# Dims-first q and k, tile-grouped recurrence products, ScalarE leaky ReLU and exponent clip in a RetNet plus feed-forward kernel

## The chip, the cores and the metric

The kernel runs on one core of a Trainium2 chip. The metric is the device time of one execution in microseconds (us). The time before the change is 878.79 us, the median of three runs (878.74 to 880.75).

## The reference

```python
B, H, S, D = 4, 8, 768, 64           # q, k, v: (B, H, S, D), float32
gamma = 1.0 - 2.0 ** (-5.0 - np.arange(H)); scale = 1.0 / np.sqrt(D)
for t in range(S):
    state = gamma[None, :, None, None] * state + np.einsum('bhd,bhe->bhde', k[:, :, t], v[:, :, t])
    y[:, :, t] = scale * np.einsum('bhd,bhde->bhe', q[:, :, t], state)
x = y.transpose(0, 2, 1, 3).reshape(B * S, H * D)   # 3072 x 512
h = x @ w_in                                        # w_in 512 x 2048, float64
g = np.maximum(0.01 * h, h)
out = (g @ w_out).astype(np.float32)                # w_out 2048 x 512, float64
```

## The kernel before

The recurrence goes by chunks of 128 tokens. A group is the same chunk `c` (0 to 5) of all four batches `b`, 512 tokens. A block, written (c, b) here, is one chunk of one batch, eight heads. The feed-forward of group c has 32 units `u` on TensorE: 16 units of `unit_h` (L200: four 128x512 products with `win`, each of which the trace shows as two passes) and 16 units of `unit_o` (L213: four parts of four products with `wout` for each batch). Between the units of group c runs the recurrence of group c + 1, one block every seven units: the decays at s = 0 (L87), the transposes at s = 1 (L98), the scores at s = 3 (L112), the outputs and the state at s = 5 (L130, L133, L141). The recurrence of group 0 stands ahead of everything.

A block does this. GpSimd multiplies q by g^t/sqrt(D) and v by g^-t. TensorE transposes q and k (four transposes each), ScalarE copies `qt` and VectorE copies `kt` out of PSUM. Eight score products use half of the array's rows each (64 dims of one head), in pairs, `a0p` and `a1p`. VectorE multiplies both results with the causal mask (`am`, L117). `yp` gets, for each of four head pairs, one 128x128 product with the block-diagonal state `st` (L130), then two products of 64 output columns with `am` (L133). ScalarE copies `yp` into `xt`. Four 128x128 products `sp` (L141) update the state, of which VectorE uses the two diagonal halves.

The weights come as float64 bits and are rounded to float32 on the chip in 32 pieces of 128x512 (16 of `win`, 16 of `wout`; p0 to p31 here). A piece takes five VectorE operations (`e` L179, `m` L186, `f` L188, `e` again L190, the result L192) and two GpSimd ones between the first and second `e` (L181, L183: clip, then shift and scale the exponent). Two pieces are rounded in each block of group 0, one behind each `unit_h` of group 0, and the last eight ahead of the `unit_o` parts that read them. The load of piece n + 4 is issued behind piece n.

The leaky ReLU of a unit is a ScalarE product with 0.01 (`low`, L203) and a VectorE maximum (`gt`, L204). All loads are issued by SyncE in program order; the scheduler is manual, so each engine runs its instructions in the order of the code. PSUM has four buffers for the recurrence (`att`), two for `hp`, two for `op`.

Of the kernel before, what the change touches and what calls it, by code (L numbers as in the profile page):

```python
# [10 lines left out]
FP32 = mybir.dt.float32  # L11
I32 = mybir.dt.int32
# [5 lines left out]
C = 128  # tokens of a chunk of the recurrence  # L18
# [3 lines left out]
def kernel(  # L22
    ctx: ExitStack,
    tc: tile.TileContext,
    q: bass.AP,
    k: bass.AP,
    v: bass.AP,
    w_in: bass.AP,
    w_out: bass.AP,
    decay: bass.AP,  # L30
    out: bass.AP,
):
# [11 lines left out]
    B, H, S, D = q.shape  # L44
    NC = S // C
    DM = H * D
    DF = w_in.shape[1]
# [4 lines left out]
    W = 512  # columns of a piece of the weights  # L52
# [14 lines left out]
    # The states of two heads, one beside the other on the diagonal; zero off it.  # L67
    st = [const.tile([128, HP, 128], FP32, name=f"st{b}") for b in range(B)]

    nc.sync.dma_start(out=dec, in_=decay)  # L70
    gq = dec[:, 0:H]
    gk = dec[:, H : 2 * H]
    gc = dec[:, 2 * H :]

# [1 line left out]
    heads = {}  # L76

    def load(c, b):
        t = [work.tile([128, H, D], FP32, tag=n, bufs=4, name=f"{n}_{c}_{b}") for n in "qkv"]
        for x, src in zip(t, (q, k, v)):  # L80
            nc.sync.dma_start(out=x, in_=src[b, :, ds(c * C, C), :].rearrange("h t d -> t h d"))
        heads[c, b] = t

    def decay_qv(c, b):
        qs, _, vs = heads[c, b]
        for x, g in ((qs, gq), (vs, gk)):
            nc.gpsimd.tensor_tensor(out=x, in0=x, in1=g.unsqueeze(2).to_broadcast([128, H, D]),  # L87
                                    op=ALU.mult)

    turned = {}  # L90

    def stage_t(c, b):
        qs, ks, _ = heads[c, b]
        got = []
        for x, n, copy in ((qs, "qt", nc.scalar.copy), (ks, "kt", nc.vector.tensor_copy)):
            ps = psum.tile([128, HP, C], FP32, tag="att", bufs=4, name=f"{n}p_{c}_{b}")
            for a in range(HP):
                nc.tensor.transpose(ps[:, a, :], x[:, 2 * a : 2 * a + 2, :], ident)  # L98
            t = work.tile([128, HP, C], FP32, tag=n, name=f"{n}_{c}_{b}")
            copy(out=t, in_=ps)  # L100
            got.append(t)
        turned[c, b] = got
# [3 lines left out]
    def stage_a(c, b):  # L106
        qt, kt = turned[c, b]
        ps = [psum.tile([128, HP, C], FP32, tag="att", bufs=4, name=f"a{j}p_{c}_{b}")
              for j in range(2)]
        for a in range(HP):  # L110
            for j in range(2):
                nc.tensor.matmul(ps[j][:, a, :], lhsT=kt[ts(j, 64), a, :],  # L112
                                 rhs=qt[ts(j, 64), a, :])
# [9 lines left out]
    def stage_y(c, b, xt):  # L123
        _, ks, vs = heads.pop((c, b))
        qt, _ = turned.pop((c, b))
        am = scores.pop((c, b))
        yp = psum.tile([128, HP, C], FP32, tag="att", bufs=4, name=f"yp_{c}_{b}")
        for a in range(HP):
            if c > 0:
                nc.tensor.matmul(yp[:, a, :], lhsT=st[b][:, a, :], rhs=qt[:, a, :],  # L130
                                 start=True, stop=False, skip_group_check=True)
            for j in range(2):
                nc.tensor.matmul(yp[ts(j, 64), a, :], lhsT=vs[:, 2 * a + j, :],  # L133
                                 rhs=am[j][:, a, :], start=(c == 0), stop=True,
                                 skip_group_check=True)
        nc.scalar.copy(out=xt[:, :, ts(b, C)], in_=yp)  # L136
        if c == NC - 1:
            return
        sp = psum.tile([128, HP, 128], FP32, tag="att", bufs=4, name=f"sp_{c}_{b}")
        for a in range(HP):  # L140
            nc.tensor.matmul(sp[:, a, :], lhsT=ks[:, 2 * a : 2 * a + 2, :],  # L141
                             rhs=vs[:, 2 * a : 2 * a + 2, :])
        for j in range(2):
            half = st[b][ts(j, 64), :, ts(j, 64)]
            new = sp[ts(j, 64), :, ts(j, 64)]
            if c > 0:
                nc.vector.tensor_tensor(out=half, in0=half, in1=new, op=ALU.add)  # L147
            nc.vector.tensor_tensor(
                out=half, in0=half if c > 0 else new,
                in1=gc[ts(j, 64)].unsqueeze(2).to_broadcast([64, HP, D]), op=ALU.mult)  # L150

# [1 line left out]
    pieces = [(w_in[ts(i, 128), ts(r, W)], win[r][i]) for r in range(DF // W) for i in range(KIN)]  # L153
    pieces += [(w_out[ts(f, 128), :], wout[f]) for f in range(KOUT)]
    first_out = KIN * (DF // W)
    raws = {}
    LOW, HIGH = 896 << 20, 1151 << 20  # float64 exponent fields of float32's 0 and 255

    def load_piece(n):
        if w_in.dtype == FP32:  # L160
            nc.sync.dma_start(out=pieces[n][1], in_=pieces[n][0])
            return
        raws[n] = work.tile([128, W], I64, tag="raw", bufs=4, name=f"raw{n}")
        nc.sync.dma_start(out=raws[n], in_=pieces[n][0])

# [6 lines left out]
    def round_words(n):  # L172
# [23 lines left out]
    def unit_h(c, f, xt):  # L196
# [27 lines left out]
    for b in range(B):  # L224
# [95 lines left out]
```

## Time and profile before

| | |
|---|---|
| median of three runs | 878.79 us |
| span of the profiled execution | 878.3 us |
| TensorE busy | 824.0 us (94%) |
| VectorE, ScalarE, GpSimd busy | 244.1, 99.5, 109.0 us |
| mean granted TensorE clock | 0.97 |
| DMA moved | 42.39 MB |

The span is the time from the first to the last instruction of the profiled execution. The median of the runs is 0.5 us longer than it. A busy TensorE is not TensorE at its peak: the records of its instructions overlap, so in the rows below the distance from start to start tells what an instruction costs. The program falls into stages: the recurrence of group 0 (to 52.8 us), the 16 `unit_h` of group 0 (to 127.6), its `unit_o` (to 229.6), and then groups 1 to 5, which are alike but for the end.

### The profile page before, as it was taken

What the parts mean: (1) busy time and instruction counts of PE and PEld (TensorE: products, weight loads), DVE (VectorE), ACT (ScalarE), POOL (GpSimd) and SP (SyncE); (2) the same over time, 40 slices, a digit from 0 to 9 for tenths busy, and PEclk for the clock granted to TensorE, in tenths of its full rate; (3) what the DMA queues carried; (4) which work ended last, traced back from release to release, by engine and by line L of the source; (5) the groups of instructions that cost most, each with busy time, mean ns of one, the idle gap of its engine ahead of it and who ended that gap; (6) DMA issues with size and microseconds to landing.
All of it is one profiled execution on the core that took longest, in us unless ns stands there. A gap on an engine that the chain in (4) does not pass through costs nothing.

```text
span 878.3 us, 6856 instructions
## 1 busy us (share of the span) xinstructions
PE 824.0 (94%) x2816; PEld 407.9 (46%) x2816; DVE 244.1 (28%) x405; ACT 99.5 (11%) x169; POOL 109.0 (12%) x119
## 2 busy tenths in 40 slices
PE   4579886699999999999999999999999999999998
PEld 3445342155455555454555454554444444444443
DVE  5878886711022211022211022210022100021000
ACT  1111110000111100111100011100011100011100
POOL 4443543620000000000000000000000000000000
PEclk9899997589999999999999999999999999999999
DMA  9864442211010111010110101110100000000000
GB/s 222 221 156 127 126 136 92 60 48 49 25 24 13 36 42 43 28 33 13 36 37 26 47 13 36 37 37 24 49 0 1 1 12 13 24 1 0 1 24 24
DMA packets 83118, 42.39 MB, mean 48 GB/s; under 512 B 75920, under 2 KB 75920, under 8 KB 83088
## 3 DMA queue, kind: packets, MB, share of 16 engines
q1 hardware_dynamic: 79632, 35.67, 16.5%
q10 hardware_dynamic: 3456, 6.29, 1.9%
q8 instruction: 22, 0.36, 0.2%
q14 instruction: 8, 0.07, 0.0%
HBM read 35.66 MB, written 6.29 MB: 48 GB/s over the span
## 4 chain that ended last, share of the span: by engine, by line
PE 83%; DVE 8%; POOL 5%; DMA 1%; issue 1%; SPq 1%; ACT 0%; POOLq 0%
PE op L213 37%; PE hp L200 32%; PE yp L133 4%; PE yp L130 3%; POOL e L183 3%; PE sp L141 2%; POOL e L181 2%; PE a0p L112 2%; DVE e L190 2%; PE qtp L98 1%; DVE win L192 1%; DVE wout L192 1%; DVE e L179 1%; PE ktp L98 1%; DVE gt L204 1%
## 5 line engine op out<-in xcount | busy, mean ns | idle before, releaser
L213 PE MATMUL op<-wout,gt 128*128 128x512 f32 x768 | 346.4, 607 | 16.5 <-DVE wout L192 16.5
L200 PE MATMUL hp<-xt,win 128*128 128x512 f32 x768 | 338.5, 596 | 0.0
L213 PEld LDWEIGHTS op<-wout,gt 128*128 128x128 f32 x768 | 145.2, 193 | 195.7 <-issue 166.9
L200 PEld LDWEIGHTS hp<-xt,win 128*128 128x128 f32 x768 | 144.0, 191 | 171.5 <-issue 169.1
L204 DVE TENSOR_TENSOR gt<-low,hp 128x512 f32<-128x512 f32 x96 | 65.9, 687 | 325.2 <-ACT low L203 325.1
L203 ACT ACTIVATE low<-hp 128x512 f32<-128x512 f32 x96 | 57.3, 597 | 301.8 <-PE hp L200 297.9
L87 POOL TENSOR_TENSOR v<-v,dec 128x512 f32<-128x512 f32 x24 | 27.7, 1153 | 266.9 <-DMA v<-in_v_dram 266.9
L133 PE MATMUL yp<-am,v 128*64 128x128 f32 x384 | 45.3, 321 | 15.8 <-DVE am L117 15.5
L87 POOL TENSOR_TENSOR q<-q,dec 128x512 f32<-128x512 f32 x24 | 28.1, 1172 | 156.1 <-DMA q<-in_q_dram 155.7
L217 ACT COPY ob<-op 128x512 f32<-128x512 f32 x24 | 14.1, 586 | 254.8 <-PE op L213 254.8
L147 DVE TENSOR_TENSOR st<-st,sp 64x256 f32<-64x256 f32 x32 | 13.4, 418 | 94.6 <-PE sp L141 94.4
L130 PE MATMUL yp<-qt,st 128*128 128x128 f32 x160 | 38.2, 321 | 0.0
L130 PEld LDWEIGHTS yp<-qt,st 128*128 128x128 f32 x160 | 26.3, 195 | 20.9 <-issue 20.9
L133 PEld LDWEIGHTS yp<-am,v 128*64 128x64 f32 x384 | 22.9, 148 | 27.6 <-issue 17.1
L117 DVE TENSOR_TENSOR am<-a0p,mask 128x512 f32<-128x512 f32 x24 | 16.5, 687 | 69.1 <-PE a1p L112 69.1
L100 DVE COPY kt<-ktp 128x512 f32<-128x512 f32 x24 | 16.5, 687 | 62.8 <-PE ktp L98 62.8
L181 POOL TENSOR_SCALAR e<-e 128x512 uint32<-128x512 uint32 x32 | 23.0, 719 | 86.8 <-DVE e L179 86.7
L112 PEld LDWEIGHTS a0p<-qt,kt 64*128 64x128 f32 x192 | 23.9, 193 | 20.1 <-issue 16.4
L112 PE MATMUL a0p<-qt,kt 64*128 64x128 f32 x192 | 28.5, 290 | 3.9 <-DVE kt L100 3.9
L188 DVE SCALAR_TENSOR_TENSOR f<-raw,m 128x512 f32<-128x512 uint32 x32 | 31.0, 970 | 1.1
L136 ACT COPY xt<-yp 128x512 f32<-128x512 f32 x24 | 14.1, 587 | 141.6 <-PE yp L133 141.6
L183 POOL TENSOR_SCALAR e<-e 128x512 uint32<-128x512 uint32 x32 | 29.6, 926 | 2.6
(27 smaller groups left out, 287.6 us busy)
## 6 DMA issues: line engine op xcount, KB each, us to landing
raw<-in_moe_w_in_dram SPq DMA_DIRECT2D x16, 512.0 KB, 5.2
raw<-in_moe_w_out_dram SPq DMA_DIRECT2D x16, 512.0 KB, 3.3
q<-in_q_dram SPq DMA_DIRECT2D x24, 256.0 KB, 3.1
k<-in_k_dram SPq DMA_DIRECT2D x24, 256.0 KB, 3.4
v<-in_v_dram SPq DMA_DIRECT2D x24, 256.0 KB, 3.9
out_dram<-ob ACTq DMA_DIRECT2D x24, 256.0 KB, 2.0
dec<-decay_dram SPq DMA_DIRECT2D x1, 10.0 KB, 1.7
```

Source lines behind the costliest of these rows:

```text
L87: nc.gpsimd.tensor_tensor(out=x, in0=x, in1=g.unsqueeze(2).to_broadcast([128, H, D]), op=ALU.mult)
L98: nc.tensor.transpose(ps[:, a, :], x[:, 2 * a : 2 * a + 2, :], ident)
L112: nc.tensor.matmul(ps[j][:, a, :], lhsT=kt[ts(j, 64), a, :], rhs=qt[ts(j, 64), a, :])
L130: nc.tensor.matmul(yp[:, a, :], lhsT=st[b][:, a, :], rhs=qt[:, a, :], start=True, stop=False, skip_group_check=True)
L133: nc.tensor.matmul(yp[ts(j, 64), a, :], lhsT=vs[:, 2 * a + j, :], rhs=am[j][:, a, :], start=(c == 0), stop=True, skip_group_check=True)
L181: nc.gpsimd.tensor_scalar(out=e, in0=e, scalar1=float(HIGH), scalar2=float(LOW), op0=ALU.min, op1=ALU.max)
L183: nc.gpsimd.tensor_scalar(out=e, in0=e, scalar1=-float(LOW), scalar2=8.0, op0=ALU.add, op1=ALU.mult)
L188: nc.vector.scalar_tensor_tensor(out=f, in0=lo, scalar=2.0 ** -32, in1=m, op0=ALU.mult, op1=ALU.add)
L200: nc.tensor.matmul(hp, lhsT=win[r][i][:, ds(o, 128)], rhs=xt[:, i, :], start=(i == 0), stop=(i == KIN - 1))
L203: nc.scalar.mul(low, hp, 0.01)
L204: nc.vector.tensor_tensor(out=gt[f], in0=low, in1=hp, op=ALU.max)
L213: nc.tensor.matmul(op, lhsT=gt[f][:, ts(b, C)], rhs=wout[f], start=(f == 0), stop=(f == KOUT - 1))
```

## The change

- q and k are also laid out with their 64 dims ahead of the tokens (`qk`, by the host), beside k and v with the tokens first (`kv`). The transposes, the identity, the copies `qt` and `kt` and the decay of q go. Each block is loaded with two transfers of 512 KB in place of three of 256 KB, into three buffers in place of four.
- The factor g^t/sqrt(D) is applied to `yp` instead, by VectorE, in the copy to `xt` (`gq` now comes in `dec`, 128x524 in place of 128x20).
- The state is kept as 128x4x64 (two heads, one on each half of the partitions). Its product with q is eight products on 64 rows and 64 columns of the array (L116), all ahead of the eight products with `am` (L121). `sp` is eight products of 64x64 outputs (L130) in place of four of 128x128. The state update is two VectorE operations on 128 partitions in place of four on 64.
- The leaky ReLU is one ScalarE operation (`AF.Prelu`). The exponent clip of a piece is two ScalarE operations (`AF.Relu`) in place of the two of GpSimd.
- Scores now stand at s = 1, outputs and state at s = 4. In group 0 both pieces of a block stand behind the scores. The weights lie contiguous by pieces.

```diff
-    def stage_t(c, b):
-        ...
-                nc.tensor.transpose(ps[:, a, :], x[:, 2 * a : 2 * a + 2, :], ident)
...
+        if c > 0:
+            for a in range(HP):
+                for j in range(2):
+                    nc.tensor.matmul(yp[ts(j, 64), a, :], lhsT=st[b][ts(j, 64), a, :],
+                                     rhs=x[ts(j, 64), 0, a, :], start=(a == 0), stop=False,
+                                     skip_group_check=True)
         for a in range(HP):
-            if c > 0:
-                nc.tensor.matmul(yp[:, a, :], lhsT=st[b][:, a, :], rhs=qt[:, a, :],
-                                 start=True, stop=False, skip_group_check=True)
             for j in range(2):
                 nc.tensor.matmul(yp[ts(j, 64), a, :], lhsT=vs[:, 2 * a + j, :],
...
-        nc.scalar.copy(out=xt[:, :, ts(b, C)], in_=yp)
+        nc.vector.tensor_tensor(out=xt[:, :, ts(b, C)], in0=yp, in1=gq, op=ALU.mult)
...
         for a in range(HP):
-            nc.tensor.matmul(sp[:, a, :], lhsT=ks[:, 2 * a : 2 * a + 2, :],
-                             rhs=vs[:, 2 * a : 2 * a + 2, :])
+            for j in range(2):
+                nc.tensor.matmul(sp[ts(j, 64), a, :], lhsT=ks[:, 2 * a + j, :],
+                                 rhs=vs[:, 2 * a + j, :], start=(a == 0), stop=True,
+                                 skip_group_check=True)
...
-        nc.gpsimd.tensor_scalar(out=e, in0=e, scalar1=float(HIGH), scalar2=float(LOW),
-                                op0=ALU.min, op1=ALU.max)
-        nc.gpsimd.tensor_scalar(out=e, in0=e, scalar1=-float(LOW), scalar2=8.0,
-                                op0=ALU.add, op1=ALU.mult)
+        nc.scalar.activation(e, e, AF.Relu, scale=-1.0, bias=float(HIGH))
+        nc.scalar.activation(e, e, AF.Relu, scale=-8.0, bias=8.0 * (HIGH - LOW))
...
-        nc.scalar.mul(low, hp, 0.01)
-        nc.vector.tensor_tensor(out=gt[f], in0=low, in1=hp, op=ALU.max)
+        nc.scalar.activation(gt[f], hp, AF.Prelu, alpha=0.01)
...
-                elif s == 5:
+                elif s == 4:
                     stage_y(c + 1, b, nx)
```

On TensorE, at block (1, 0), between two units of group 0, before:

```order
L200 MATMUL hp_5_604<-xt_164,win_3_76 128x512
L130 MATMUL yp_0_624<-qt_0_521,st_117 128x128
L133 MATMUL yp_0_624<-am_1_0_580,v_0_240 64x128
L133 MATMUL yp_0_624<-am_1_0_582,v_0_240 64x128
L130 MATMUL yp_0_624<-qt_0_521,st_117 128x128
L133 MATMUL yp_0_624<-am_1_0_580,v_0_240 64x128
L133 MATMUL yp_0_624<-am_1_0_582,v_0_240 64x128
```

and now, at the same block, one unit earlier:

```order
L183 MATMUL hp_4_484<-xt_143,win_3_75 128x512
L116 MATMUL yp_0_502<-qk_0_266,st_116 64x128 x8
L121 MATMUL yp_0_502<-am_1_0_444,kv_0_267 64x128
L121 MATMUL yp_0_502<-am_1_0_446,kv_0_267 64x128
...
L130 MATMUL sp_0_520<-kv_0_267 64x64 x8
L183 MATMUL hp_5_535<-xt_143,win_0_72 128x512
```

The state products stood in turn with those of `am`; now all eight stand together ahead of them, and `sp` follows with products as narrow as these.

On ScalarE, at the first two units of group 0, where `low` and the copy `qt` stood alone before:

```order
L203 ACTIVATE low_0_479<-hp_0_474 128x512
L203 ACTIVATE low_1_501<-hp_1_496 128x512
L100 COPY qt_0_521<-qtp_0_516 128x512
L203 ACTIVATE low_2_535<-hp_2_530 128x512
L203 ACTIVATE low_3_555<-hp_3_550 128x512
```

and now:

```order
L185 ACTIVATE gt_100<-hp_0_397 128x512
L166 ACTIVATE e_403<-e_403 128x512
L167 ACTIVATE e_403<-e_403 128x512
L185 ACTIVATE gt_101<-hp_1_416 128x512
L166 ACTIVATE e_422<-e_422 128x512
L167 ACTIVATE e_422<-e_422 128x512
```

The two clips of a piece now stand in ScalarE's queue behind the leaky ReLU of the unit ahead of it.

On VectorE, in the last eight pieces of `wout` (p27 is `wout_95`, p28 begins with `e_890`), now:

```order
L164 TENSOR_SCALAR e_841<-raw_780 128x512
...
L173 SCALAR_TENSOR_TENSOR e_841<-raw_780,e_841 128x512
L175 SCALAR_TENSOR_TENSOR wout_95<-f_843,e_841 128x512
L124 TENSOR_TENSOR xt_396<-yp_2_857,dec 128x4x128
L134 TENSOR_TENSOR st_118<-st_118,sp_2_875 128x256
L135 TENSOR_TENSOR st_118<-st_118,dec 128x256
L164 TENSOR_SCALAR e_890<-raw_815 128x512
```

Before, p24 to p31 stood in one row there; now block (1, 2)'s three operations, which wait for TensorE, stand between the first four and the last four.

## Rows read from the trace of the kernel before

**Rows 1.** Busy us (and instructions) by stage: PE, PEld, DVE, ACT, POOL, PEclk, DMA, GB/s.
```profile
0.00:52.80 52.80, 27.30 (x193) 23.26 (x194) 37.82 (x63) 5.97 (x9) 24.05 (x31) 0.90 0.91 214
52.80:127.60 74.80, 69.45 (x242) 33.70 (x240) 61.74 (x104) 11.30 (x19) 29.21 (x32) 0.98 0.48 132
127.60:229.60 102.00, 82.20 (x242) 38.27 (x242) 39.52 (x64) 4.71 (x9) 30.71 (x32) 0.80 0.20 58
229.60:364.30 134.70, 134.70 (x481) 66.99 (x480) 25.17 (x44) 16.26 (x29) 8.34 (x8) 1.00 0.13 32
...
633.70:764.80 131.10, 131.10 (x449) 63.41 (x448) 18.46 (x28) 16.26 (x28) 0.00 (x0) 1.00 0.02 8
764.80:878.30 113.50, 109.85 (x256) 48.27 (x255) 11.02 (x16) 12.48 (x21) 0.00 (x0) 1.00 0.03 12
```

**Rows 2.** Timeline of TensorE, one block of group 2: start us, us, what [idle before].
```profile
370.96 0.60 PE L98 MATMUL qtp<-ident,q 128*128 128x128 f32 x4
...
371.83 7.03 PE L200 MATMUL hp<-xt,win 128*128 128x512 f32 x16
...
379.01 0.27 PE L112 MATMUL a0p<-qt,kt 64*128 64x128 f32 x1
379.02 0.27 PE L112 MATMUL a1p<-qt,kt 64*128 64x128 f32 x1
379.12 0.27 PE L112 MATMUL a0p<-qt,kt 64*128 64x128 f32 x1
...
379.89 7.13 PE L200 MATMUL hp<-xt,win 128*128 128x512 f32 x16
386.86 0.38 PE L130 MATMUL yp<-qt,st 128*128 128x128 f32 x2
387.17 0.44 PE L133 MATMUL yp<-am,v 128*64 128x128 f32 x4
387.54 0.49 PE L130 MATMUL yp<-qt,st 128*128 128x128 f32 x2
...
389.91 1.16 PE L141 MATMUL sp<-v,k 128*128 128x128 f32 x8
390.90 5.32 PE L200 MATMUL hp<-xt,win 128*128 128x512 f32 x12
```

**Rows 3.** Timeline of VectorE and GpSimd, one piece of `wout` and the next's start.
```profile
143.00 0.42 DVE L179 TENSOR_SCALAR e<-raw 128x512 uint32<-128x512 uint32 x1
...
143.79 0.98 DVE L188 SCALAR_TENSOR_TENSOR f<-raw,m 128x512 f32<-128x512 uint32 x1
144.31 0.94 POOL L183 TENSOR_SCALAR e<-e 128x512 uint32<-128x512 uint32 x1
145.28 0.69 DVE L190 SCALAR_TENSOR_TENSOR e<-raw,e 128x512 uint32<-128x512 uint32 x1 [0.51 <-POOL e L183]
...
146.61 0.42 DVE L179 TENSOR_SCALAR e<-raw 128x512 uint32<-128x512 uint32 x1
```

**Rows 4.** Group by line: busy us, mean ns | idle before, releaser.
```profile
L203 ACT ACTIVATE low<-hp 128x512 f32<-128x512 f32 x96 | 57.3, 597 | 301.8 <-PE hp L200 297.9
```

**Rows 5.** Timeline of VectorE in group 0's recurrence.
```profile
8.53 0.43 DVE L179 TENSOR_SCALAR e<-raw 128x512 uint32<-128x512 uint32 x1
...
26.79 0.68 DVE L117 TENSOR_TENSOR am<-a0p,mask 128x512 f32<-128x512 f32 x1
...
27.98 0.42 DVE L179 TENSOR_SCALAR e<-raw 128x512 uint32<-128x512 uint32 x1
...
37.55 0.68 DVE L117 TENSOR_TENSOR am<-a0p,mask 128x512 f32<-128x512 f32 x1
```

**Rows 6.** Busy us by stretch around the end of the last pieces, columns as in rows 1.
```profile
143.00:173.00 30.00, 14.76 (x15) 3.74 (x16) 25.09 (x41) 0.00 (x0) 15.66 (x18) 0.53 0.26 79
173.00:182.00 9.00, 9.00 (x35) 5.75 (x36) 0.01 (x1) 1.17 (x2) 5.61 (x6) 0.50 0.08 29
182.00:190.00 8.00, 8.00 (x19) 3.51 (x19) 1.67 (x4) 0.00 (x0) 1.04 (x1) 0.99 0.30 66
```

More of the change, by code (lines that the diff above doesn't have):

```diff
@@ L7 @@
 from concourse.bass import ds, ts
-from concourse.masks import make_identity
 from concourse._compat import with_exitstack
 FP32 = mybir.dt.float32
-I32 = mybir.dt.int32
 U32 = mybir.dt.uint32
@@ L18 @@
 C = 128
+W = 512
 @with_exitstack
@@ L24 @@
     tc: tile.TileContext,
[L25 to L29, printed above, removed]
+    qk: bass.AP,
+    kv: bass.AP,
+    weights: bass.AP,
     decay: bass.AP,
     out: bass.AP,
+    B: int,
+    H: int,
+    S: int,
+    D: int,
+    DF: int,
 ):
     nc = tc.nc
-    B, H, S, D = q.shape
     NC = S // C
     DM = H * D
-    DF = w_in.shape[1]
     HP = H // 2
@@ L51 @@
     N = B * C
-    W = 512
+    f64 = weights.dtype == I64
     ctx.enter_context(tc.manual_schedule())
@@ L66, with decay_v @@
     gt = [const.tile([128, N], FP32, name=f"gt{f}") for f in range(KOUT)]
[L68 to L73, printed above, removed]
+    st = [const.tile([128, HP, D], FP32, name=f"st{b}") for b in range(B)]
+    gq = dec[:, 0 : HP * C].rearrange("p (a t) -> p a t", t=C)
+    gk = dec[:, HP * C : HP * C + H]
+    gc = dec[:, HP * C + H :]
     heads = {}
     def load(c, b):
[L79 to L90, printed above, removed]
-    def stage_t(c, b):
[L93 to L97, printed above, removed]
-                nc.tensor.transpose(ps[:, a, :], x[:, 2 * a : 2 * a + 2, :], ident)
[L99 to L102, printed above, removed]
+        x = work.tile([128, 2, HP, C], FP32, tag="qk", bufs=3, name=f"qk_{c}_{b}")
+        y = work.tile([128, 2, H, D], FP32, tag="kv", bufs=3, name=f"kv_{c}_{b}")
+        nc.sync.dma_start(out=x, in_=qk[c, b])
+        nc.sync.dma_start(out=y, in_=kv[c, b])
+        heads[c, b] = x, y
+    def decay_v(c, b):
+        v = heads[c, b][1][:, 1]
+        nc.gpsimd.tensor_tensor(out=v, in0=v, in1=gk.unsqueeze(2).to_broadcast([128, H, D]),
+                                op=ALU.mult)
     scores = {}
     def stage_a(c, b):
-        qt, kt = turned[c, b]
+        x = heads[c, b][0]
         ps = [psum.tile([128, HP, C], FP32, tag="att", bufs=4, name=f"a{j}p_{c}_{b}")
@@ L143, in stage_y @@
[L143 to L153, printed above, removed]
@@ L154 @@
-    pieces += [(w_out[ts(f, 128), :], wout[f]) for f in range(KOUT)]
+            for j in range(2):
+                nc.tensor.matmul(sp[ts(j, 64), a, :], lhsT=ks[:, 2 * a + j, :],
+                                 rhs=vs[:, 2 * a + j, :], start=(a == 0), stop=True,
+                                 skip_group_check=True)
+        if c > 0:
+            nc.vector.tensor_tensor(out=st[b], in0=st[b], in1=sp, op=ALU.add)
+        nc.vector.tensor_tensor(out=st[b], in0=st[b] if c > 0 else sp,
+                                in1=gc.unsqueeze(2).to_broadcast([128, HP, D]), op=ALU.mult)
@@ L155 @@
+    pieces = [win[r][i] for r in range(DF // W) for i in range(KIN)] + wout
     first_out = KIN * (DF // W)
@@ L159, in load_piece @@
     def load_piece(n):
-        if w_in.dtype == FP32:
-            nc.sync.dma_start(out=pieces[n][1], in_=pieces[n][0])
+        if not f64:
+            nc.sync.dma_start(out=pieces[n], in_=weights[n])
             return
         raws[n] = work.tile([128, W], I64, tag="raw", bufs=4, name=f"raw{n}")
-        nc.sync.dma_start(out=raws[n], in_=pieces[n][0])
+        nc.sync.dma_start(out=raws[n], in_=weights[n])
     def round_piece(n):
-        if w_in.dtype == I64:
+        if f64:
             round_words(n)
@@ L191, in round_words @@
                                        op0=ALU.bitwise_and, op1=ALU.bitwise_or)
-        nc.vector.scalar_tensor_tensor(out=pieces[n][1], in0=f, scalar=2.0 ** -20,
+        nc.vector.scalar_tensor_tensor(out=pieces[n], in0=f, scalar=2.0 ** -20,
                                        in1=e.bitcast(FP32), op0=ALU.mult, op1=ALU.mult)
@@ L222, in new_xt, with load_ahead @@
         return work.tile([128, KIN, N], FP32, tag="xt", name=f"xt_{c}")
-    for b in range(B):
-        load(0, b)
-        load_piece(b)
-    make_identity(nc, ident)
+    def load_ahead(c, b):
+        n = c * B + b + 3
+        if n < NC * B:
+            load(*divmod(n, B))
+    load(0, 0)
+    nc.sync.dma_start(out=dec, in_=decay)
+    load_piece(0)
+    load_piece(1)
+    load(0, 1)
+    load_piece(2)
+    load_piece(3)
+    load(0, 2)
     nc.vector.memset(mask, 1.0)
@@ L230 @@
                             base=0, pattern=[[1, 128]], channel_multiplier=-1)
-    for b in range(B):
-        nc.vector.memset(st[b], 0.0)
     done = 0
     x = new_xt(0)
-    decay_qv(0, 0)
     for b in range(B):
-        stage_t(0, b)
-        if b + 1 < B:
-            decay_qv(0, b + 1)
+        decay_v(0, b)
+        stage_a(0, b)
         round_piece(done)
-        stage_a(0, b)
         round_piece(done + 1)
@@ L245 @@
         stage_y(0, b, x)
-        load(1, b)
+        load_ahead(0, b)
     for c in range(NC):
@@ L316 @@
     with tile.TileContext(nc) as tc:
-        kernel(tc, *args)
+        kernel(tc, *args, B, H, S, D, DF)
     r = run_bass_kernel_spmd(nc, [arrays], core_ids=[0])
```

59 lines of the change are left out of this document (36 added, 23 removed).

## The prediction

> **What bounds the kernel now.** I read the busy times by stage first [rows 1]. From 229.6 us to the end TensorE is busy without a gap at granted clock 1.00: three groups of 134.7 us, one of 131.1 (whose blocks have no state update), and 113.5 for the last, which has no recurrence beside it. Ahead of that lie three stages in which TensorE waits: 27.3 busy of 52.8 us in group 0's recurrence, 69.5 of 74.8 in its `unit_h`, 82.2 of 102.0 (clock 0.80) in its `unit_o`. There VectorE and GpSimd round the weights. So there are two questions: what does TensorE spend on a block where it is the bound, and at what pace does a piece get rounded where it isn't. The first I read in the timeline of TensorE across one block [rows 2], from start to start; the second in the timeline of VectorE across one piece [rows 3].
>
> **A block on TensorE, before.** One 512-column pass takes 109.85 / 256 = 0.429 us [rows 1]. A block's seven units (56 passes) take 24.0 us. The transposes take 371.83 - 370.96 = 0.87 [rows 2]. From the `unit_h` behind them, 16 x 0.429 = 6.86 ends at 378.69; the next begins at 379.89 and loses another 0.11 before the state products at 386.86 start. So the scores cost 1.31 [rows 2]. Outputs and state cost 390.90 - 386.86 = 4.04. In sum 6.22 beside the units.
>
> **A block on TensorE, after.** The transposes go: -0.87. The scores are the same eight pairs: no change. For the new outputs I need three prices. A pair of half-array products starts every 0.11 (379.01 and 379.02 together, the next at 379.12), as fast as one full pass, so a pair costs one. A change of tiling costs what is left over: the two pairs with `am` stand from 387.17 to 387.54, 0.37, of which 0.22 are pairs, so about 0.16 [rows 2]. Before, each of four head pairs paid that twice; now the change is paid entering the state products, entering those with `am`, and going back to the units. The eight pairs of state passes: 8 x 0.11 + 0.16 = 1.04. With `am`: 1.04. `sp`: no row has 64-column products; between 0.055 a pair (half the columns of a 0.11 pair) and 0.11 (no gain from narrowness), 0.44 to 0.88; I take 0.44, since the pass times above go by columns. Back: 0.16. Sum 2.68 against 4.04. A block saves 0.87 + 1.36 = 2.23. One without `sp`: the old one costs 6.22 - 3.6 / 4 = 5.32 [rows 1], the new 1.31 + 2.24 = 3.55; it saves 1.77.
>
> From 229.6 on stand 12 blocks of the first kind (groups 2, 3, 4) and four of the second: 12 x 2.23 + 4 x 1.77 = **33.8 us**. The last group changes nothing.
>
> **The pace of a piece.** Before, 146.61 - 143.00 = 3.61 us, with VectorE idle 0.51 for GpSimd's second clip [rows 3]; without that wait VectorE needs 3.10. Now ScalarE clips. An operation of this size takes it 0.597 [rows 4] (from PSUM, in float; no row shows 32-bit integers from SBUF; between 0.6 and the 0.94 that GpSimd took [rows 3], I take 0.6, the row of the same engine). The first `e` ends 0.42 behind its start; two clips and three hand-overs of 0.03 to 0.05 (GpSimd's ends at 145.25, VectorE goes on at 145.28) end at 1.77; `e` again and the result take 146.61 - 145.28 = 1.33: 3.10. Both ways 3.1.
>
> **Group 0's recurrence.** VectorE sets it: a block took 37.55 - 26.79 = 10.76 [rows 5]. It now has two masks (27.98 - 26.79 = 1.19), two pieces (6.2), the multiply to `xt` (0.60, as a mask), the state (0.35): 8.34. The first piece began at 8.53 [rows 5]; ahead of p0 there are now 1.3 MB in place of 0.8, so I put it at 9 (8 to 11). Four blocks later, less the first masks and the last state step, the units begin at 9 + 33.4 - 1.5 = **41 us** against 52.8.
>
> **Group 0's `unit_h`.** A unit takes TensorE 3.43, a piece 3.1, and each piece is read four or more units after it is rounded, so TensorE sets it, unless ScalarE's order does. The clips of a piece wait in ScalarE's queue behind the leaky ReLU, and that for TensorE: the rounding can't run ahead of TensorE any more, but it needn't. Behind the clips wait the next leaky ReLU, and behind that the third `hp` buffer's unit; 0.6 + 1.3 of 3.43 are taken, so nobody waits. The maximum that VectorE no longer does (16 x 0.6) is covered, as are the masks and multiplies of two blocks: at no cost while 3.1 + (2 x 2.5) / 16 stays under 3.43 + (2 x 3.99) / 16. The decay of q, ahead of which the transposes stood, is gone. So 16 x 3.43 + 2 x (1.31 + 2.68) + 1 for a half-clock start = **64 us** against 74.8.
>
> **Group 0's `unit_o`.** Eight pieces remain. From the last `unit_h`: p23 3.4 (leaky ReLU 0.6, clips 1.3, `e` again and the result 1.33, hand-overs), masks 1.2, p24 to p27 12.4: 17.0. TensorE follows its last product of part 2 at half clock (it stood at 0.53 in the like stretch [rows 6]), 18.7; outputs and state of block (1, 2) at half clock, then the multiply and state steps: 24.3. Only then come p28 to p31, since these steps stand ahead of them on VectorE: 36.7, the last product 38.5. The move to s = 4 costs that wait of about 7 us; but the scores at s = 1 save the like ahead of p24. The rest is 12 units x 3.43 and block (1, 3), 3.99: 45.2, and 3 for the clock, which came back only at 182, 9 us behind the last piece [rows 6]. Sum **87 us** against 102.0.
>
> **What costs nothing.** The loads: 25 MB in place of 19 for q, k and v, in transfers of long rows; three buffers reach three blocks ahead, over 60 us in the steady groups. On SyncE a block's load now waits for TensorE's outputs of that block, and the next piece's load stands behind it; pieces are loaded four ahead, 12 us, which covers that, and if it didn't, VectorE would wait for `raw`. In group 0's recurrence a block needs 2.1 MB in 8.3 us, 250 GB/s, where 214 were moved [rows 1]; I take it as covered by the longer rows, and price it below. ScalarE loses two copies, VectorE gains the multiply: both idle over 100 of 134.7 us there [rows 1]. The leaky ReLU moved to ScalarE alone: worth nothing in the steady groups for the same reason.
>
> By the Trainium skill (ScalarE: Activation LUTs, Rules for kernel authors) relu and max belong on VectorE, which it puts at up to about three times ScalarE's speed in bf16. Here, in float32, ScalarE's 0.597 stands beside VectorE's 0.68 for a mask [rows 4, 5], and VectorE is the engine that is short; the sum goes by the rows.
>
> **The sum.** Units of group 1 begin at 41 + 64 + 87 = 192 against 229.6: 37.6. With the 33.8: 878.3 - 71.4 = 806.9 for the span, and 0.5 more for the median of the runs: **807 us**.
>
> **Rivals.** First, the state products don't pair. The old pairs of row halves wrote two tiles, `a0p` and `a1p`; the new ones write two partition halves of one, `yp`. If they go one by one, 8 x 0.11 = 0.88 more in all 20 blocks: 17.6 us, **825**. For pairing speaks that the column halves with `am` already write one tile side by side (0.37 for four passes, [rows 2]). By the Trainium skill (TensorEngine Tiling (Array Packing), Restrictions and Gotchas) different row tiles can't access the same PSUM bank at the same time; taken to the letter that is this rival, and no row here has row halves in one tile. Chance 0.13.
>
> Second, ScalarE is slow on integers: 0.94 a clip makes a piece 3.8. Sixteen pieces outside `unit_h` cost 0.7 each, 11, and in `unit_h` the piece overtakes the unit by about 0.2, 3 more: **821**. Chance 0.12.
>
> Third, the loads bound the start: at 214 GB/s a block of group 0 takes 9.8, 1.5 more, and the first piece 1 later: 7 us, **814**. Chance 0.07.
>
> Slower: the packed half-array stretch lets the clock fall at every block. The place is each of the 20 blocks that TensorE sets; the price that of [rows 6], 9 us at 0.50 with TensorE busy throughout, 4.5 a block, 90 in all: **897**. It turns slower than before from 71.4 / 20 = 3.6 a block. Against it: a steady block has half-array scores and outputs already, at clock 1.00 [rows 1]. Chance 0.02. That the change does less than it says, the steady blocks gaining only their transposes (0.87 x 20), would be 834: 0.03, since the switches it removes are in the rows.
>
> **How the numbers follow.** The forecast itself has 0.63: with `sp` at 0.88 (+6), the first piece 2 later or 1 earlier, and the clock stretches between none (-4) and twice as priced (+4), it spans 799 to 818. The range reaches to the first three rivals: **798 to 826**, which leaves out under 0.2. A measurement of this kernel tells about 0.3% from no change; faster by that is every case but the clock's: 0.97; within it 0.01; slower 0.02.
>
> **What would show it.** Steady groups of 134.7 - 4 x 2.23 = 125.8 us, the state products starting in pairs 0.11 apart; a piece every 3.1 us with VectorE waiting for ScalarE hardly at all; the first unit at 41 us; no TensorE gap among the 16 `unit_h`; a gap in `unit_o` around p28. State passes 0.11 apart one by one show the first rival, ScalarE clips of 0.9 the second, VectorE waiting for `raw` the third, a clock under 1.00 after 200 us the fourth. It would be wrong above all if ScalarE's order held TensorE up.

## The result and the profile after

The changed kernel takes 810.5 us (median of four runs, 809.4 to 812.0) against 878.8 for the kernel before: 0.922 of its time, 95% interval 0.920 to 0.924. The forecast was 807, with 798 to 826 as its range. Busy time by stage of the changed kernel, columns as in [rows 1]:

```profile
0.00:42.60 42.60, 20.15 (x193) 17.84 (x193) 34.11 (x57) 11.37 (x17) 7.71 (x11) 0.72 0.76 293
42.60:107.60 65.00, 65.00 (x258) 31.14 (x260) 48.23 (x87) 26.42 (x46) 3.71 (x3) 0.97 0.48 168
107.60:192.50 84.90, 71.54 (x257) 32.67 (x258) 30.74 (x55) 13.55 (x22) 2.13 (x2) 0.88 0.22 72
192.50:318.30 125.80, 125.80 (x513) 60.89 (x513) 10.93 (x20) 11.89 (x20) 4.17 (x4) 1.00 0.13 42
570.00:694.00 124.00, 124.00 (x450) 58.67 (x449) 7.92 (x12) 11.89 (x20) 1.04 (x1) 1.00 0.05 17
694.00:807.50 113.50, 109.89 (x257) 48.38 (x255) 0.00 (x0) 12.48 (x21) 0.00 (x0) 1.00 0.03 12
```

Beside [rows 1], group 0's recurrence went from 52.8 to 42.6 us, its `unit_h` from 74.8 to 65.0 without a gap on TensorE, its `unit_o` from 102.0 to 84.9; a steady group from 134.7 to 125.8, the one without a state update from 131.1 to 124.0. The last group is unchanged.

The two gaps that `unit_h` had before were waits of the transposes for GpSimd's decay of q (kernel before):

```profile
61.57 0.66 PE L98 MATMUL qtp<-ident,q 128*128 128x128 f32 x4 [1.76 <-POOL q L87]
...
95.61 0.66 PE L98 MATMUL qtp<-ident,q 128*128 128x128 f32 x4 [3.58 <-POOL q L87]
```

One block on TensorE at the full clock, (1, 3), to set beside [rows 2] (timeline: start, us, line, operation, tiles, count):

```profile
158.60 10.57 PE L194 MATMUL op<-wout,gt 128*128 128x512 f32 x24
169.10 1.09 PE L116 MATMUL yp<-qk,st 64*64 64x128 f32 x16
170.12 1.09 PE L121 MATMUL yp<-am,kv 128*64 128x128 f32 x16
171.05 0.64 PE L130 MATMUL sp<-kv 128*64 128x64 f32 x16
171.61 1.12 PE L194 MATMUL op<-wout,gt 128*128 128x512 f32 x2
```

From start to start the state products take 1.02, those with `am` 0.93 and `sp` with the way back 0.56: 2.51. The change of tiling that enters the state products lies ahead of them: the 24 passes from 158.60 to 169.10 take 10.50, where 24 x 0.429 is 10.30. With these 0.20 the block takes 2.71; the prediction counted 2.68. The blocks of the steady groups have the same three steps (the first of group 1, from 210.86 on).

The pieces on VectorE, as [rows 3] had them (in brackets the idle time before, and its releaser):

```profile
118.14 0.42 DVE L164 TENSOR_SCALAR e<-raw 128x512 uint32<-128x512 uint32 x1
118.93 0.69 DVE L171 SCALAR_TENSOR_TENSOR f<-raw,m 128x512 f32<-128x512 uint32 x1
119.92 0.69 DVE L173 SCALAR_TENSOR_TENSOR e<-raw,e 128x512 uint32<-128x512 uint32 x1 [0.29 <-ACT e L167]
120.64 0.69 DVE L175 SCALAR_TENSOR_TENSOR wout<-f,e 128x512 f32<-128x512 f32 x1
121.25 0.42 DVE L164 TENSOR_SCALAR e<-raw 128x512 uint32<-128x512 uint32 x1
...
129.42 0.69 DVE L124 TENSOR_TENSOR xt<-yp,dec 128x512 f32<-128x512 f32 x1 [4.97 <-PE yp L121]
```

A piece takes 121.25 - 118.14 = 3.11 us. The last row (`xt`) is block (1, 2)'s multiply, at which VectorE waits 4.97 us for TensorE with the last four pieces queued behind it.

### The profile page after: what moved, and what is told of

It reads as the page before. It is cut to its first block, busy times and chain, and to the rows that moved or that the text cites. A ratio compares the mean times of both kernels' runs of the same rounds, so it can differ in the third digit from the quotient of the medians.

```text
span 807.5 us, 6705 instructions
## 1 busy us (share of the span) xinstructions
PE 768.1 (95%) x2944; PEld 371.5 (46%) x2944; DVE 153.8 (19%) x269; ACT 111.4 (14%) x185; POOL 27.1 (3%) x29
## 4 chain that ended last, share of the span: by engine, by line
PE 90%; DVE 6%; ACT 2%; DMA 1%; issue 0%; SPq 0%
PE hp L183 42%; PE op L194 40%; PE yp L116 3%; PE yp L121 3%; PE a0p L97 2%; DVE e L173 1%; ACT e L167 1%; ACT e L166 1%; PE sp L130 1%; DVE wout L175 1%; DMA raw<-in_weights_dram 1%; DVE e L164 1%; DVE win L175 1%; DVE am L102 1%; DVE f L171 1%; DVE xt L124 0%
## 5 line engine op out<-in xcount | busy, mean ns | idle before, releaser
L185 ACT ACTIVATE gt<-hp 128x512 f32<-128x512 f32 x96 | 57.3, 597 | 298.2 <-PE hp L183 298.2
L86 POOL TENSOR_TENSOR kv<-kv,dec 128x512 f32<-128x512 f32 x24 | 26.6, 1108 | 568.1 <-DMA kv<-in_kv_dram 563.0
L121 PE MATMUL yp<-am,kv 128*64 128x128 f32 x384 | 31.6, 304 | 13.7 <-issue 12.5
L97 PEld LDWEIGHTS a0p<-qk 64*128 64x128 f32 x192 | 25.4, 203 | 19.8 <-issue 14.6
L97 PE MATMUL a0p<-qk 64*128 64x128 f32 x192 | 30.2, 302 | 4.3 <-DMA qk<-in_qk_dram 4.3
L121 PEld LDWEIGHTS yp<-am,kv 128*64 128x64 f32 x384 | 24.4, 150 | 19.0 <-issue 16.5
L97 PE MATMUL a1p<-qk 64*128 64x128 f32 x192 | 30.2, 302 | 0.0
L166 ACT ACTIVATE e<-e 128x512 uint32<-128x512 uint32 x32 | 20.1, 627 | 50.6 <-DVE e L164 50.5
L173 DVE SCALAR_TENSOR_TENSOR e<-raw,e 128x512 uint32<-128x512 uint32 x32 | 22.6, 705 | 19.6 <-ACT e L167 19.6
L97 PEld LDWEIGHTS a1p<-qk 64*128 64x128 f32 x192 | 25.4, 203 | 0.0
L116 PEld LDWEIGHTS yp<-qk,st 64*64 64x64 f32 x320 | 17.7, 137 | 15.9 <-issue 15.2
L116 PE MATMUL yp<-qk,st 64*64 64x128 f32 x320 | 22.6, 282 | 0.0
L167 ACT ACTIVATE e<-e 128x512 uint32<-128x512 uint32 x32 | 20.2, 630 | 1.0
```

The source lines that it names most:

```text
L86: nc.gpsimd.tensor_tensor(out=v, in0=v, in1=gk.unsqueeze(2).to_broadcast([128, H, D]), op=ALU.mult)
L97: nc.tensor.matmul(ps[j][:, a, :], lhsT=x[ts(j, 64), 1, a, :], rhs=x[ts(j, 64), 0, a, :])
L116: nc.tensor.matmul(yp[ts(j, 64), a, :], lhsT=st[b][ts(j, 64), a, :], rhs=x[ts(j, 64), 0, a, :], start=(a == 0), stop=False, skip_group_che ...
L166: nc.scalar.activation(e, e, AF.Relu, scale=-1.0, bias=float(HIGH))
L167: nc.scalar.activation(e, e, AF.Relu, scale=-8.0, bias=8.0 * (HIGH - LOW))
L173: nc.vector.scalar_tensor_tensor(out=e, in0=hi, scalar=0x80000000, in1=e, op0=ALU.bitwise_and, op1=ALU.bitwise_or)
```

## Experiments

Each edit is made on the changed kernel unless the text says otherwise, and each time stands against its 810.5 us. "The theory" and "the rival" are those of the expectation above the result. The runs stand on several chips, on which the kernel before took 878.8 to 880.3 us in the median; so 1 to 2 us between two kernels tell nothing, and differences of 3 to 4 us rest on the stage times given with them.

**The clips back on GpSimd.**

```diff
-        nc.scalar.activation(e, e, AF.Relu, scale=-1.0, bias=float(HIGH))
-        nc.scalar.activation(e, e, AF.Relu, scale=-8.0, bias=8.0 * (HIGH - LOW))
+        nc.gpsimd.tensor_scalar(out=e, in0=e, scalar1=float(HIGH), ...)
+        nc.gpsimd.tensor_scalar(out=e, in0=e, scalar1=-float(LOW), ...)
```

> The changed kernel with the two clips of a piece back on GpSimd, nothing else undone. Theory (the pace of a piece fell because VectorE no longer waits for the clips): a piece takes 3.6 us again in place of 3.1, with VectorE idle about 0.5 in each; 16 pieces lie outside group 0's unit_h, so 8 us longer, 816 to 821; inside unit_h TensorE still sets the pace and its 65 us stay. Rival (the start got shorter because VectorE lost the maximum and the copies, whoever clips): a piece is no slower where it counts, 0 to 2 us.

818.1 us, 7.6 longer, as the theory had it. The first unit starts 4.2 us later (46.74), `unit_o` is 4.1 longer, and VectorE waits 0.51 for GpSimd in a piece again. Its `f` is slow again too. `f` in this kernel and in the changed one (minimum, median, maximum in ns, first and last start):

```profile
L173 DVE SCALAR_TENSOR_TENSOR f<-raw,m x32: 978/979/981, 9.3 to 149.0; 128x512 f32<-128x512 uint32 x32
```

```profile
L171 DVE SCALAR_TENSOR_TENSOR f<-raw,m x32: 691/693/1579, 8.7 to 141.3; 128x512 f32<-128x512 uint32 x32
```

**The leaky ReLU back on both engines.**

```diff
-        nc.scalar.activation(gt[f], hp, AF.Prelu, alpha=0.01)
+        low = work.tile([128, N], FP32, ...)
+        nc.scalar.mul(low, hp, 0.01)
+        nc.vector.tensor_tensor(out=gt[f], in0=low, in1=hp, op=ALU.max)
```

> The changed kernel with the leaky ReLU back as a ScalarE product and a VectorE maximum. Theory (the move is worth nothing, since TensorE covers VectorE in unit_h and in the steady groups): 0 to 2 us longer, unit_h of group 0 stays at 65 us, steady groups at 125.85. Rival (VectorE is the bound in unit_h): 16 maxima of 0.6 us there, 10 us longer.

814.5 us: 4.0 longer, and neither was right. TensorE has no gap in `unit_h`, so the cover (VectorE's work hidden behind TensorE's) did hold there. From the first unit to the start of the last pass of `unit_h` it takes 65.2 us (43.27 to 108.42) in place of 64.4 (42.56 to 106.91). These 0.8 lie in the first 16 passes, which take 9.68 in place of 8.91. But from that last pass on, `unit_o` takes 89.5 us in place of 85.4. VectorE in this kernel:

```profile
109.51 0.42 DVE L164 TENSOR_SCALAR e<-raw 128x512 uint32<-128x512 uint32 x1
...
112.63 0.68 DVE L187 TENSOR_TENSOR gt<-low,hp 128x512 f32<-128x512 f32 x1
113.22 0.42 DVE L164 TENSOR_SCALAR e<-raw 128x512 uint32<-128x512 uint32 x1
...
117.54 0.42 DVE L164 TENSOR_SCALAR e<-raw 128x512 uint32<-128x512 uint32 x1
```

and p24 in the changed kernel:

```profile
111.91 0.42 DVE L164 TENSOR_SCALAR e<-raw 128x512 uint32<-128x512 uint32 x1
```

A piece with the maximum takes 113.22 - 109.51 = 3.71, more than a unit's 3.43, so VectorE ends `unit_h` behind. Its p24 (the last row of the first view) starts 9.1 us after the start of the last pass of `unit_h`, where the changed kernel has 5.0. The debt, the time by which VectorE is behind, is 4.1 us and is paid in the next stage. Two more runs below test this reading.

**State and `am` products in turn for each head pair**, as before, but still half-array.

```diff
-        if c > 0:
-            for a in range(HP):
+        for a in range(HP):
+            if c > 0:
                 for j in range(2): ...   # state
-        for a in range(HP):
             for j in range(2): ...       # am
```

> The changed kernel with the half-array state products and the products with the masked scores in turn for each head pair, as before the change, instead of grouped. Theory (a change of tiling costs about 0.16 us, and grouping removes six of them a block): 0.96 us a block, 20 blocks, 19 us longer, steady groups 3.8 us longer at 129.7. Rival (the gain of the outputs came from the narrower products, not from the grouping): no change.

829.3 us: 18.8 longer, as the theory had it. A block in this kernel's timeline of TensorE:

```profile
173.00 0.43 PE L116 MATMUL yp<-qk,st 64*64 64x128 f32 x4
173.37 0.44 PE L120 MATMUL yp<-am,kv 128*64 128x128 f32 x4
173.74 0.43 PE L116 MATMUL yp<-qk,st 64*64 64x128 f32 x4
...
175.84 0.63 PE L129 MATMUL sp<-kv 128*64 128x64 f32 x16
```

Two pairs (four passes) take 0.37 with their change of tiling. The same products take 175.84 - 173.00 = 2.84 in place of 1.95: 0.15 for each of the six changes more.

**A full 128x128 state**, block-diagonal, four full products in place of eight half ones, still grouped. VectorE's state update is four operations on 64 partitions again.

```diff
-                for j in range(2):
-                    nc.tensor.matmul(yp[ts(j, 64), a, :], lhsT=st[b][ts(j, 64), a, :], ...)
+                nc.tensor.matmul(yp[:, a, :], lhsT=st[b][:, a, :], ...)
```

> The changed kernel with the state as a block-diagonal 128x128 again, its four full-array products grouped ahead of the others. Theory (the half-array pairs take as long as the full products they replace; only the number of tiling changes counts): the full products need no change of tiling behind the units, 0.16 us less a block, 3 us shorter in TensorE; VectorE's two more state steps cost up to 2 us in group 0; in all 3 us shorter to 1 us longer. Rival (the pairs on half the array save half of the state products' time): 0.88 us a block, 17 us longer.

811.0 us, 0.5 longer: no difference that the two sets of runs can tell. Four full products cost about what eight pairs cost (0.98 us from start to start in place of 1.02); the gain lies in the grouping, not in the narrow state. The trace shows both halves of the theory: from group 1 on this kernel is 1.8 us shorter (613.4 in place of 615.2), and group 1 starts 2.2 us later (194.50 in place of 192.31).

**q and k turned on the chip again**, the transposes one unit ahead of the scores.

```diff
+    def stage_t(c, b):
+        ...
+        for i, (src, copy) in enumerate(((qs, nc.scalar.copy), (y[:, 0], nc.vector.tensor_copy))):
+            ps = ...
+            for a in range(HP):
+                nc.tensor.transpose(ps[:, a, :], src[:, 2 * a : 2 * a + 2, :], ident)
+            copy(out=x[:, i], in_=ps)
```

> The changed kernel with q and k turned on the chip again: loaded tokens first, eight transposes a block one unit ahead of the scores, copied out by ScalarE and VectorE; the rest as in the change. Theory (the transposes lay on TensorE's path with their full 0.87 us a block): 20 blocks in stretches that TensorE sets, 17 us longer, steady groups 3.5 us longer at 129.3; and 2 to 6 us more in group 0's recurrence, where VectorE gets a copy of 0.6 a block and the scores wait for it: 829 to 835. Rival (the transposes fitted beside other work, and what the change gained in the steady groups is the regrouping alone): no more than 6 us longer.

830.9 us: 20.3 longer, as the theory had it. A steady group takes 129.35 in place of 125.85, 0.88 a block; the other third lies ahead of group 1, whose first unit starts 7.6 us later. `unit_h` of group 0 has no gap here either: with the transposes back but no decay of q ahead of them, the two waits of the kernel before are gone.

**The outputs and state of block (1, 2) one unit later.**

```diff
-                elif s == 4:
+                elif s == (5 if (c, b) == (0, 2) else 4):
```

> The changed kernel with the outputs and state of block (1, 2) one unit later, behind the last part of the first batch's unit_o, so that VectorE rounds p24 to p31 without a wait for TensorE between p27 and p28. The wait it saves is 5.0 us in the trace and the multiply and state steps 1.4. Theory (the block must still be done, then at half clock, about 3.6 us, and no longer beside rounding): 2 to 4 us shorter. Rival (the wait is a cost by itself, as the prediction priced it): 6 to 7 us shorter.

807.4 us: 3.1 shorter, as the theory had it. VectorE's 4.97 us between p27 and p28 are gone, and p24 to p31 follow each other at 3.12, but the block still has to be done, now behind p31.

**The exponent one piece ahead.** The first `e` and both clips of piece n + 1 are issued ahead of the last two operations of piece n.

```diff
+    def exponent(n):
+        ...                      # e and both clips of piece n, once
     def round_words(n):
+        exponent(n)
         ...                      # m, f
+        exponent(n + 1)
         ...                      # e again, result
```

> The changed kernel with the first operation of the next piece (and so its clips) issued ahead of the last two of a piece. Theory (a piece takes 3.1 us because VectorE waits for the two clips in a chain; VectorE's own work is about 2.75, now that f runs at 0.69 with GpSimd idle): a piece 2.75 to 2.8, 16 pieces outside unit_h, 5 to 6 us shorter, 804 to 806. Rival (VectorE's own five operations are the 3.1, as the prediction's other way of counting had it): no change.

801.8 us: 8.7 shorter, as the theory had it but with more gain than its 5 to 6. VectorE in this kernel:

```profile
113.05 0.42 DVE L179 TENSOR_SCALAR m<-raw 128x512 uint32<-128x512 uint32 x1
...
114.45 0.69 DVE L184 SCALAR_TENSOR_TENSOR e<-raw,e 128x512 uint32<-128x512 uint32 x1
115.17 0.69 DVE L186 SCALAR_TENSOR_TENSOR wout<-f,e 128x512 f32<-128x512 f32 x1
115.78 0.42 DVE L179 TENSOR_SCALAR m<-raw 128x512 uint32<-128x512 uint32 x1
```

A piece takes 2.73 and waits for nothing. Of the gain, only 0.7 us come ahead of the first unit, where VectorE now waits 0.86 and 1.07 for `raw`; the rest is in group 0's `unit_o`. There the clock adds to it: the product ahead of block (1, 2) and its state products take 2.07 us (from 121.38) where they took 3.78 in the changed kernel (from 124.50), and VectorE's wait ahead of p28 falls from 4.97 to 3.27.

**The leaky ReLU back on both engines, with the exponent ahead** (the edits of the second and the seventh run together).

> The kernel with the exponent taken one piece ahead (801.8 us), with the leaky ReLU put back to ScalarE's multiply and VectorE's maximum. In the changed kernel that step cost 4.0 us, and the theory on it is a backlog: with 3.71 a piece VectorE is slower than TensorE's 3.43 a unit, so the pieces lag at the end of group 0's unit_h and all of unit_o starts late. With the exponent ahead a piece takes 2.73 and the maximum 0.6 more, 3.33, under the 3.43, so no backlog is left: 802 to 803.5, and the first operation of p24 stands no more than 1 us later behind the last unit_h than without the maximum. The rival: the cost is the maximum itself, its place in VectorE's queue behind a wait for TensorE or its hand-over at each unit; then it stays, 805 to 807.

810.8 us: 9.0 above the 801.8, and neither number held. VectorE in this kernel:

```profile
61.38 0.69 DVE L198 TENSOR_TENSOR gt<-low,hp 128x512 f32<-128x512 f32 x1 [0.52 <-ACT low L197]
61.98 0.42 DVE L179 TENSOR_SCALAR m<-raw 128x512 uint32<-128x512 uint32 x1
...
65.31 0.69 DVE L198 TENSOR_TENSOR gt<-low,hp 128x512 f32<-128x512 f32 x1 [0.52 <-ACT low L197]
65.92 0.42 DVE L179 TENSOR_SCALAR m<-raw 128x512 uint32<-128x512 uint32 x1
```

The two queues wait for each other in a ring. The maximum waits for ScalarE's multiply, which stands behind the clips of the next piece, which wait for an `e` that VectorE issues behind the last maximum. A step is 65.92 - 61.98 = 3.94, above the 3.43 again.

**The same with the maximum in the middle of the piece**, where the multiply has been done.

```diff
         ...                      # m, f of piece n
+        maximum()                # of the unit just issued (group 0 only)
         exponent(n + 1)
```

> The exponent one piece ahead and the leaky ReLU on ScalarE's multiply and VectorE's maximum, as in the run before (810.8), but in group 0 the maximum stands in the middle of the piece, after f and before the next piece's e, where the multiply has long been done. The theory: what costs is a VectorE step per unit longer than TensorE's 3.43, so that the pieces end unit_h behind. In the run before the step was 3.93: 2.73 for the piece, 0.60 for the maximum, and 0.52 to 0.60 in which the maximum waited for ScalarE's multiply, which stood behind the clips of the next piece's e. Without the wait the step is 3.33: p24's mantissa starts within 1 us of where it does without the maximum (110.3) and the time is 802 to 803.5. The rival: the maximum costs by itself, wherever it stands, at least the 4.0 us that it cost in the changed kernel: 805.8 or more.

807.7 us: 3.2 better than the ring, but 5.8 above the 801.8, so the theory's number fell and the rival's held. The trace splits the 5.8 (5.6 between the two profiled spans). Away from the blocks a step is 3.33, as expected. But 0.1 under TensorE's 3.43 leaves no room for anything else: VectorE still waits at 98.2 (for `low`, and so for TensorE), has no pause from there on (one mantissa stretched to 1.27 and a block's two masks lie in between), and starts p24 at 112.46 in place of 110.32, 2.1 late. The clock then more than doubles that. TensorE around the last product of p27, first without the maximum (exponent ahead), then with it:

```profile
121.38 1.12 PE L205 MATMUL op<-wout,gt 128*128 128x512 f32 x2 [1.60 <-DVE wout L186]
122.43 1.09 PE L116 MATMUL yp<-qk,st 64*64 64x128 f32 x16
123.45 1.09 PE L121 MATMUL yp<-am,kv 128*64 128x128 f32 x16
```

```profile
123.51 2.07 PE L215 MATMUL op<-wout,gt 128*128 128x512 f32 x2 [1.60 <-DVE wout L189]
125.51 1.97 PE L116 MATMUL yp<-qk,st 64*64 64x128 f32 x16
127.42 1.98 PE L121 MATMUL yp<-am,kv 128*64 128x128 f32 x16
```

The same three steps run at the half clock, so VectorE gets `yp` 4.84 us later (129.44 against 124.60) and finishes the last piece 4.84 later: 2.13 of debt and 2.71 of clock. Another 0.8 is lost behind it. Why the clock had fallen at 123.5 in the one and not at 121.4 in the other is open; the idle time just before both is 1.60.

**The decay of v left out.**

```diff
-        decay_v(0, b)
...
-                    decay_v(c + 1, b)
```

> GpSimd's decay of v is left out altogether (the keys' values go into the state undecayed); all else as in the changed kernel. The theory: the blocks of group 0's recurrence take 8.8 to 9.5 us in place of the predicted 8.34 because each decay (1.04 to 1.59 us on GpSimd) stretches the VectorE operation that it meets. Five such operations stand ahead of the first unit in the changed kernel: f 1.58 in place of 0.69, m 1.26 and 1.27 in place of 0.42, win 1.41 in place of 0.69, e 1.16 in place of 0.42; 4.0 us in sum. Then the first unit starts at 38.5 to 40 us (now 42.6), no mask or mantissa operation of group 0's recurrence takes over 0.8, and the time is 806 to 808 (now 810.5). The rival: the stretched operations come from the loads (293 GB/s in that stage), which stay; then the long operations are still there and the time is within 1 us of 810.5.

807.2 us: 3.4 shorter, as the theory had it (the two profiled spans differ by 1.8). VectorE, where a block's first pieces run (`xt` of blocks 0 to 2 of group 0):

```profile
14.58 0.68 DVE L124 TENSOR_TENSOR xt<-yp,dec 128x512 f32<-128x512 f32 x1
...
22.93 0.68 DVE L124 TENSOR_TENSOR xt<-yp,dec 128x512 f32<-128x512 f32 x1
...
31.29 0.68 DVE L124 TENSOR_TENSOR xt<-yp,dec 128x512 f32<-128x512 f32 x1
```

A block takes 8.35, and no operation there is stretched. The first unit starts at 40.4 (forecast 38.5 to 40): p0 came 0.4 later in this run, and part of the stretches had lain in the 0.29 that VectorE waits for ScalarE anyway.

**The rounding spread out.** With the exponent ahead: one piece in each block of group 0, five for each four `unit_h`, the last eight together, and the first two batches' `unit_o` take parts 0 to 2 before either's part 3. The loads at the start are reordered to match.

```diff
-        round_piece(done + 1)
-        done += 2
+        done += 1
...
+    FIRST = [(0, 0), (0, 1), (0, 2), (1, 0), (1, 1), (1, 2), (0, 3), (1, 3)]
...
-                round_piece(done)
-                done += 1
+                for _ in range(2 if u % 4 == 1 else 1): ...
```

> As the run before, and the pieces spread: one in each block of group 0, five for every four unit_h, the last eight together; the first two batches' unit_o take their first three parts before either's last. Theory (the start is bound by VectorE's sum, some 115 us for 32 pieces and the first blocks, once TensorE has other work while it waits): the first unit at 27 to 32 us, the units of group 1 at 152 to 165 in place of 192, 768 to 783 in all. Rival (ScalarE's order, with the clips behind a leaky ReLU that waits for TensorE, or the loads hold the rounding up): no first unit before 35 us or a unit_h stage over 75 us, and 790 to 805.

779.9 us (777.1 to 781.3), 0.886 of the kernel before, 95% interval 0.882 to 0.890: within the theory's 768 to 783. Its first stages, columns as above:

```profile
0.00:30.50 30.50, 15.97 (x192) 13.97 (x192) 20.61 (x38) 7.60 (x11) 5.72 (x10) 0.94 0.90 338
30.50:93.10 62.60, 62.58 (x255) 30.39 (x256) 59.27 (x107) 31.76 (x53) 4.97 (x4) 1.00 0.60 209
93.10:161.60 68.50, 65.45 (x258) 31.34 (x257) 28.64 (x54) 12.42 (x20) 2.26 (x2) 0.98 0.27 89
```

TensorE starts its units 12 us earlier, VectorE fills `unit_h` (59.27 of 62.6), and `unit_o` has 3 us of gaps left at clock 0.98 in place of 13 at 0.88. At the start the loads now cost time: DMA is 0.90 busy, and VectorE waits 3.0 us for `raw`. What the spreading, the order of the parts and the order of the loads give one by one is not tested.

## Why the prediction was right

**The steady blocks: right, by the steps given.** Predicted 2.23 saved a block, measured (134.7 - 125.8) / 4 = 2.2. The parts hold one by one: 0.87 for the transposes (0.88 a block when they came back), about 0.16 a change of tiling (0.15 in the interleaved run), `sp` at half the price of a 128-column pair (0.56 with the way back; predicted 0.44 + 0.16). The group without `sp`: 124.0, as 131.1 - 4 x 1.77 gives.

**The pace: right in size, by one of its two countings.** Predicted 3.10, measured 3.11. But only the chain through ScalarE is 3.1: VectorE waits 0.29 at the second `e`, so its own work had shrunk below that. `f` had fallen from 0.98 [rows 3] to 0.69 once GpSimd's clips were gone, which "both ways 3.1" missed. With the chain taken apart the piece takes 2.73.

**Group 0's recurrence: 42.6 against 41.** The failed term is the block, 8.34: it took 8.8 to 9.5. Five of the six decays of v that GpSimd does ahead of the first unit stretch the VectorE operation that they meet, as two pairs of rows show (VectorE, then GpSimd):

```profile
17.12 1.26 DVE L169 TENSOR_SCALAR m<-raw 128x512 uint32<-128x512 uint32 x1
...
22.87 1.41 DVE L175 SCALAR_TENSOR_TENSOR win<-f,e 128x512 f32<-128x512 f32 x1
```

```profile
16.95 1.16 POOL L86 TENSOR_TENSOR kv<-kv,dec 128x512 f32<-128x512 f32 x1 [4.08 <-DMA kv<-in_kv_dram]
...
22.14 1.59 POOL L86 TENSOR_TENSOR kv<-kv,dec 128x512 f32<-128x512 f32 x1 [4.04 <-DMA kv<-in_kv_dram]
```

Undisturbed these take 0.42 and 0.69. Without the decay a block takes 8.35: the sum was right but for this. The early start of the first piece (7.9, predicted 9) took part of it back. Of the 10.2 us that this stage gained, the runs put about 4.2 down to the clips (first unit at 46.74 with them back) and 2.1 to the transposes (44.61); the rest, with the decay of q, the state steps and the loads, is not taken apart.

**Group 0's `unit_h`: 65.0 against 64**, with no gap, as predicted. The 16 passes of the first two units take 8.91 us where 6.87 is the full clock: 2 us for the start where 1 was counted. The gaps went with the decay of q, as the prediction had it: they stay away when the transposes, the clips or the maximum come back.

**Group 0's `unit_o`: 84.9 against 87.** The wait that the move to s = 4 puts ahead of p28 is there: 4.97, predicted about 7. The block was expected at half clock throughout; its state products did run at it (1.77 from start to start), but those with `am` were back at 0.93. After the last piece the clock reads 0.84 from 143.8 to 158.7, and 1.00 from there.

**What was wrong: "at no cost" for the maximum.** The cover was computed as an average over `unit_h`, 3.41 against 3.93, and TensorE indeed never waited there. But the 3.41 leaves out the maximum that it was to show covered: with it, at 3.71 a piece, the average is 4.02, already above 3.93. And VectorE's work doesn't end with the stage. A piece with the maximum is 3.71 against 3.43 in the units that carry no block, and what VectorE is behind at the end delays the last eight pieces, which bound the next stage. So the move to one ScalarE operation was worth 4 us. The time forecast didn't suffer: its 87 for `unit_o` counts without such a debt, and the changed kernel has none.

**Errors that cancelled.** That the sum came so near is in part luck. The stages missed by +1.6, +1 and -2, and the profiled span, 807.5, lies 0.6 above the 806.9 worked out. The rest of the 3.5 us by which the median misses: a run's time lies 1.9 us above its span here, not 0.5 (that figure set one execution's span against the median of others), and the profiled run is the fastest of the four, 1.1 under the median.

**The rivals.** The state products pair: two starts stand 7 ns apart and the next two follow 0.109 later, and all sixteen passes take 1.02, so the first rival is refuted for two halves of one `yp`. The rule of the Trainium skill (TensorEngine Tiling (Array Packing), Restrictions and Gotchas) on row tiles and one PSUM bank does not hold as it stands for this diagonal pair; by it a block would have cost 0.88 more. ScalarE's clip on integers takes 0.63, not the second rival's 0.94:

```profile
L166 ACT ACTIVATE e<-e x32: 621/630/632, 8.4 to 141.0; 128x512 uint32<-128x512 uint32 x32
```

The third, loads that bound the start, is refuted too: 293 GB/s were moved, and VectorE waited for `raw` 0.2 us in all (0.7 to 1.9 in three of the runs above). The fourth, the clock: 1.00 in every steady group.

## What to carry to other kernels

Products of unlike tilings are worth grouping even where each is small: a change cost about 0.15 us here, and six more of them in each of 20 blocks cost 18.8; narrowing the state products brought nothing. Cover has to be checked with the work that is to be covered in the sum, and in the last stretch of a stage and not only on its average, because an engine that ends a stage behind delays whatever binds the next one, and a TensorE that waits may then run the delayed work at half clock too. Where two engines hand one tile back and forth, issue the first half of the next item ahead of the second half of this one, but look at what else waits in the second engine's queue: behind the early half stood the multiply, and the ring cost 3.2 us on top of the 5.8 that the maximum cost without it.

## What the chip showed that was not expected

- A GpSimd operation on SBUF can hold up the VectorE operation beside it: `f` at 11.83 took 1.58 beside a decay from 11.82 to 12.86. The five that met a decay ahead of the first unit ended 0.55 us behind it if they take 0.69 alone, and 0.28 if they take 0.42, as if most of their work came after it. The masks at 6.44 and 7.05, which read PSUM, kept their 0.69 and 0.68 beside the decay at 6.49. The Trainium skill (SBUF — State Buffer, Who interferes with whom) has a port pair that the two engines lock for a whole instruction; these rows agree, and so does `f` at 0.69 without and 0.98 with GpSimd's clips.
- A change of clock multiplies a delay: 2.1 us of late work became 4.8 where TensorE had meanwhile fallen to its lower level, 1.2 GHz.
- Eight pairs of 64-column products start 0.058 us apart, close to half of the 0.109 of 128 columns; four full 128x128 products cost what eight half-array pairs cost (0.98 and 1.02).
